# Fused attention and SwiGLU block: the front of batches 0 and 1 reordered, with VectorE sums for two denominators

## The chip, the core and the metric

The kernel runs on one core of a Trainium2 chip. A core has five engines with instruction queues of their own: TensorE (PE: matmuls and, beside them, weight loads, PEld), VectorE (DVE), ScalarE (ACT), GpSimd (POOL) and SyncE (SP). Each works its queue in order; an instruction starts when its turn has come and when everything that it waits for is there. Transfers run on 16 DMA engines beside them. Nearly all loads here are issued by POOL, since they turn fp32 into bf16 on the way. The metric is the device time of one execution in microseconds (us); less is better.

## The reference

Eight batches of attention over a compressed memory, then a SwiGLU block. Sizes: 8 batches, 8 heads, 576 positions, head size 64, 32 memory slots; 512 model columns, 1536 hidden columns.

```python
a = np.exp(phi - max)                     # [b, h, s, m]
a = a / (a.sum(axis=s) + 1e-09)           # weights of the 32 memory slots
k_m = einsum('bhsm,bhsd->bhmd', a, k)     # compressed keys
v_m = einsum('bhsm,bhsd->bhmd', a, v)     # compressed values
p = softmax(scale * q @ k_m.T)            # over the 32 slots
x = (p @ v_m) as [4608, 512]
out = (silu(x @ w_gate) * (x @ w_val)) @ w_out
```

The denominators of the first softmax can be divided out late (into the scale of the score exponential and of the evacuation of U, below), and so can the maximum be left out.

## The kernel before

**Front.** Batches 0 and 1 are prepared by code written out by hand at the end of the kernel (L880 to L960), in program order for all engines. `phi_exp_masked` writes exp(phi) into a tile `t_mphi` that holds two groups g of partitions, each with zeros in the other's half. `k_items` gives two steps: `denominators` (18 matmuls of one column with a vector of ones, L244, then a reciprocal L262 and its product with the scale, L352, the tile `rk`) and `sums` (36 matmuls L325 by `direct`, then four copies to `t_kT`, L339). `q_items` transposes q on TensorE in three parts (L383), copied to `t_qT` by the engine that a letter names, "v" for VectorE and "a" for ScalarE. `scores` (L396) is followed by four exponentials on ScalarE (L407, scale `rk`). The inverse sum of the second softmax is made by `z_inv` (a matmul L423 with the block matrix `bones`, then Ln, Ln, Exp on ScalarE, L426 and L428). Later batches use another form, `z_inv_v`: on VectorE a transposing sum L435, a reciprocal L442, a transpose L444. `norm` multiplies the exponentials by it (L452, the tile `t_A`). `v_direct` makes the values' part of `t_kT`. `warm(n)` issues matmuls of `bones` with itself (L870, 512 columns each for n = 4) whose results nobody reads, to keep TensorE busy while it would wait.

**Into the hidden layer.** A matmul of the compressed values with a chunk of w_gate or w_val gives U (L472, `u_round`), which is evacuated from PSUM by ScalarE (L494) and VectorE (L498). `gv_gate` multiplies U's gate half with `t_A` (L515, 2 matmuls of 288 columns) and puts Silu on ScalarE (L532); the postponed `mul` does the same with the value half and multiplies on VectorE (L538). `flush_mul(n)` issues n of the postponed ones. `gv_slot` is a gate, then the values that were pending. The hidden columns come in three chunks of 512; chunk 0 comes in two halves ("half chunks" 0 and 1), because its weights are loaded in halves. `u_half(b, which, 0, half, evac)` makes U for half a chunk, with which = (0,) for gates, (1,) for values, (0, 1) for both; evac names the engines for the two PSUM banks.

**Loads.** POOL issues in this order: k0, q0, k1, q1, v0, v1, the weights W of chunk 0 in quarters (gate, value, gate, value), chunk 1 (gate, value), chunk 2 (gate, value), then w_out's first chunk (WO), k2, WO, phi2, WO, v2. phi0 and phi1 are issued by SP and ACT.

**PSUM.** There are 8 banks, handed out from a list in program order: `bank` takes the first, `done` puts one at the end. A matmul therefore also waits until the last reader of its bank has finished.

Of the kernel before, what the change touches and what calls it, by code (L numbers as in the profile page):

```python
# [9 lines left out]
FP32 = mybir.dt.float32  # L10
BF16 = mybir.dt.bfloat16
# [3 lines left out]
def kernel(  # L15
# [135 lines left out]
    def load_wo(c):  # L151
        t = wpool.tile([128, 4, DM], BF16, tag=f"WO{c}", name=f"WO{c}")
        nc.gpsimd.dma_start(
            out=t,
            in_=moe_w_out[c * CH:(c + 1) * CH, :].rearrange("(i p) f -> p i f", p=128),
        )
        for i in range(4):
            WO[4 * c + i] = t[:, i]
        WOc[c] = t


    ident = consts.tile([128, 128], BF16, tag="ident", name="ident")
    bones = consts.tile([128, 128], BF16, tag="bones", name="bones")
    ones1 = consts.tile([128, 1], BF16, tag="ones1", name="ones1")
    ones2 = consts.tile([128, NG], BF16, tag="ones2", name="ones2")


    ephis, rSs, bkvs, kTs, es, atts = {}, {}, {}, {}, {}, {}
# [10 lines left out]
    masked = {}  # L179
# [23 lines left out]
    esums = {}  # L203

    def phi_sum(b):
# [13 lines left out]
        nc.gpsimd.tensor_tensor(out=hl[:, 1], in0=t[:, 0], in1=hl[:, 0], op=ALU.subtract)  # L219
        esums[b] = hl  # L220

    def kv_sum(b, p, parts):


        w0, w1 = parts[0], parts[-1] + 1
        n = (w1 - w0) * D
        for j in range(JK):
            for i in range(NP):
                for g in range(NG):
                    nc.tensor.matmul(  # L230
                        p[g][32 * i:32 * i + 32, 0:n],
                        lhsT=phi_of(b, g, j, i),
                        rhs=kvs[b][64 * g:64 * g + 64, w0:w1, i, j * D:(j + 1) * D],
                        start=(j == 0),
                        stop=(j == JK - 1),
                        tile_position=(64 * g, 32 * i),
                    )

    def kv_denominators(b, p):

        if b in masked:
            for g in range(NG):
                for j in range(JK):
                    nc.tensor.matmul(  # L244
                        p[:, g:g + 1],
                        lhsT=masked[b][:, j, g].rearrange("p i m -> p (i m)"),
                        rhs=ones1,
                        start=(j == 0),
                        stop=(j == JK - 1),
                    )  # L250
            return
        if b in esums:
            hl = esums.pop(b)
            terms = [hl[:, t] for t in range(2)]
        else:
            terms = [ephis[b][:, j].rearrange("p i m -> p (i m)") for j in range(JK)]
        for n, x in enumerate(terms):
            nc.tensor.matmul(p, lhsT=x, rhs=ones2, start=(n == 0), stop=(n == len(terms) - 1))
# [157 lines left out]
    lzs = {}  # L416

    def z_inv(b, g):

        p = gv_banks()  # L420
        lz = att.tile([128, 2, HALF], FP32, tag="lz", bufs=3, name="t_lz")
        for r in range(2):
            nc.tensor.matmul(  # L423
                p[r][:, 0:HALF], lhsT=bones, rhs=es[b, g][:, r], start=True, stop=True
            )
            nc.scalar.activation(out=lz[:, r], in_=p[r][:, 0:HALF], func=AF.Ln)  # L426
        done(*p)
        nc.scalar.activation(out=lz, in_=lz, func=AF.Exp, scale=-1.0)  # L428
        lzs[b, g] = lz
# [17 lines left out]
        )  # L447
        lzs[b, g] = lz

    def norm(b, g):  # L450
        a = att.tile([128, 2, HALF], BF16, tag=f"A{g}", name="t_A")
        nc.vector.tensor_tensor(out=a, in0=es.pop((b, g)), in1=lzs.pop((b, g)), op=ALU.mult)  # L452
        atts[b, g] = a


# [49 lines left out]
    def flush_mul(n=None):  # L505
        for _ in range(len(pend) if n is None else n):
            pend.pop(0)()
# [316 lines left out]
    def q_items(b, evac):  # L824
        return [lambda n=n: q_T(b, n, evac[n]) for n in range(3)]
# [5 lines left out]
    def u_half(b, which, c, half, evac):  # L831

        return lambda: u_round(b, ((which, c, (half,)),), evac)
# [9 lines left out]
    def run(items):  # L843
        for x in items:
            x()
# [13 lines left out]
    def gv_slots(b):  # L859
        return [lambda s=s: gv_slot(b, s) for s in range(2 * NJF)]  # L860

    def warm(n, narrow=0):


        p = bank([128, DM], FP32, "p_warm")
        x = bones.rearrange("p (a c) -> p a c", a=1)
        sizes = [1] * narrow + [4] * ((n - narrow) // 4)
        sizes += [n - sum(sizes)] if n > sum(sizes) else []
        for a in sizes:
            nc.tensor.matmul(  # L870
                p[:, 0:128 * a],
                lhsT=bones,
                rhs=x.to_broadcast([128, a, 128]) if a > 1 else bones,
                start=True,
                stop=True,
            )
        free.insert(0, held.pop(id(p))[0])
# [6 lines left out]
    load_q(0)  # L884
    load_k(1)
    nc.vector.memset(bones, 0.0)
    nc.vector.memset(ones1, 1.0)
    nc.vector.memset(ones2, 0.0)
    for g in range(NG):
        nc.vector.memset(ones2[64 * g:64 * g + 64, g:g + 1], 1.0)  # L890
# [12 lines left out]
    for c in range(1, NCH):  # L903
        for which in range(2):
            load_w(which, c)
    load_wo(0)
    load_k(2)
    load_wo(1)
    load_phi(2, nc.gpsimd)
    load_wo(2)  # L910
    load_v(2)
    for c in range(NCH):
        u_buffer(1, c, f"S{c}")


    warm(104)
    k0, k1 = k_items(0, "vvvv"), k_items(1, "vvvv")
    q0, q1 = q_items(0, "vav"), q_items(1, "vav")
    run(k0)
    warm(8)  # L920
    run(k1[:1])
    run(q0)
    warm(4)
    scores(0, 0)
    scores(0, 1)
# [1 line left out]
    z_inv(0, 0)  # L927
    run(k1[1:])
    z_inv(0, 1)
    norm(0, 0)  # L930
    warm(12)
    run(q1)
    norm(0, 1)
    warm(8)
    scores(1, 0)
# [1 line left out]
    v_direct(0, "vvvv")  # L937
    z_inv(1, 0)
    warm(8)
    z_inv(1, 1)  # L940
    norm(1, 0)
    warm(16)
    v_direct(1, "vvvv")
    warm(8)
# [1 line left out]

    g0, g1 = gv_slots(0), gv_slots(1)
    nc.scalar.preload_act_table_set("silu_and_others")
    run([u_half(0, (0,), 0, 0, "va")])
    norm(1, 1)  # L950
    run([u_half(0, (1,), 0, 0, "va"), u_half(1, (0, 1), 0, 0, "av")])
    for s in range(4):
        gv_gate(0, s)
    flush_mul(2)
    for s in range(2):
        gv_gate(1, s)
        flush_mul(1)
    run([u_half(0, (0, 1), 0, 1, "va"), u_half(1, (0, 1), 0, 1, "aa")])
    flush_mul(2)
    run(g1[2:4] + g0[4:8] + g1[4:6])  # L960
    for c in range(1, NCH):
        s = 8 * c
        run([u_item(0, c)] + g1[s - (2 if c == 1 else 3):s] + g0[s:s + 5])
# [27 lines left out]
    for b in range(2, B):  # L991
# [59 lines left out]
        g = gv_slots(b)  # L1051
# [61 lines left out]
```

## Time and profile before

| what | value |
|---|---|
| median of the 3 runs shown | 232.75 us (232.64 to 232.76) |
| the profiled execution's own time | 232.59 us |
| its span, first to last instruction | 230.8 us |
| TensorE busy in the span | 222.3 us (96%) |
| VectorE, ScalarE, GpSimd busy | 184.8 us, 171.6 us, 145.1 us |
| read from and written to HBM | 42.47 MB, 9.44 MB |
| granted TensorE clock, mean | 1.000 |

How to read the profile: busy shares are means over the whole span, and the stages differ. A row of the timeline has the start, the length, the engine, the line, the operation, the tiles (out<-in), the shape and the number of instructions; in brackets stands how long the engine was idle before it, and what ended that. "issue" means that nothing in the profile shows the cause. "DMA to landing" is the time from a transfer's issue to the arrival of its last byte. Matmuls overlap one another, so their lengths don't add up; their distance from start to start does.

### The profile page before, as it was taken

Reading aid. Unit: us, or ns where it says so; the run is one execution under the profiler, and the core shown is the slowest. Engines: PE = TensorE matmul, PEld = TensorE weight load, DVE = VectorE, ACT = ScalarE, POOL = GpSimd, SP = SyncE. Lnnn points to the kernel's source line nnn. Section 1 sums busy time; section 2 is a strip of 40 time slices with the busy share of each in tenths; the row PEclk is TensorE's granted clock in tenths of the full one; section 3 lists DMA queues with packets and bytes.
Section 4 is the critical chain, followed back from the end, with each engine's and each line's share of the span. In section 5 each row is a group of like instructions: output and inputs, shape, how many; then the busy total and the mean of one; then the engine's idle time right before and its main releaser. Section 6 shows DMA issues by size and latency. Waiting matters only on the chain.

```text
span 230.8 us, 7191 instructions
## 1 busy us (share of the span) xinstructions
PE 222.3 (96%) x2818; PEld 169.7 (74%) x2818; DVE 184.8 (80%) x423; ACT 171.6 (74%) x365; POOL 145.1 (63%) x197
## 2 busy tenths in 40 slices
PE   6997799999999999999999999999999999999993
PEld 2554476778887777878788787887788778878882
DVE  4056789999976799989997668998999899977832
ACT  2858898988547989968896658978898789677310
POOL 8422427998099759765977689464845394029291
PEclk9999999999999999999999999999999999999999
DMA  6999999999996993999299964996022602202024
GB/s 213 209 211 206 199 207 207 216 250 266 207 210 176 258 257 69 224 204 177 78 214 195 230 137 110 253 231 101 18 76 102 116 0 95 87 7 91 23 93 162
DMA packets 36546, 36.84 MB, mean 160 GB/s; under 512 B 14496, under 2 KB 30880, under 8 KB 36512
## 3 DMA queue, kind: packets, MB, share of 16 engines
q0 software_dynamic: 16272, 22.42, 52.7%
q1 hardware_dynamic: 19712, 13.37, 22.8%
q10 hardware_dynamic: 528, 0.59, 0.8%
q8 instruction: 22, 0.36, 0.6%
q14 instruction: 12, 0.10, 0.1%
HBM read 42.47 MB, written 9.44 MB: 225 GB/s over the span
## 4 chain that ended last, share of the span: by engine, by line
PE 87%; DMA 9%; POOL 2%; issue 0%; DVE 0%; POOLq 0%
PE p_os L723 21%; PE p_g L515 21%; PE p_v L515 20%; PE p_oc L723 10%; DMA W<-in_moe_w_val_dram 9%; PE p_oa L723 5%; PE p_u L472 5%; PE p_kv L230 2%; PE p_g L396 1%; POOL t_kv L99 1%; POOL t_kv L103 1%; PE p_q L383 1%; POOL t_q L108 0%; POOL W L138 0%; DVE t_q L339 0%
## 5 line engine op out<-in xcount | busy, mean ns | idle before, releaser
L538 DVE TENSOR_TENSOR t_h<-t_sg,p_v 128x288 bf16<-128x288 bf16 x192 | 81.7, 451 | 14.3 <-PE p_v L515 7.3
L515 PEld LDWEIGHTS <-t_U 128*128 128x128 bf16 x768 | 73.9, 98 | 21.2 <-issue 3.5
L532 ACT ACTIVATE t_sg<-p_g 128x288 bf16<-128x288 f32 x192 | 73.2, 424 | 17.2 <-PE p_g L515 11.4
L515 PE MATMUL p_g<-t_A,t_U 128*128 128x288 bf16 x384 | 77.0, 286 | 0.0
L515 PE MATMUL p_v<-t_A,t_U 128*128 128x288 bf16 x384 | 76.9, 286 | 0.0
L723 PEld LDWEIGHTS <-t_S 128*128 128x128 bf16 x384 | 37.3, 98 | 4.5 <-issue 0.2
L603 POOL TENSOR_TENSOR t_S<-t_h 128x512 bf16<-128x512 bf16 x17 | 19.6, 1154 | 27.7 <-DVE t_h L538 26.4
L723 PEld LDWEIGHTS <-t_h 128*128 128x128 bf16 x288 | 27.1, 98 | 8.6 <-issue 5.0
L492 ACT CAST t_U<-p_u 128x512 bf16<-128x512 f32 x51 | 27.0, 606 | 6.4 <-PE p_u L472 6.4
L723 PE MATMUL p_os<-t_T,t_S 128*128 128x256 bf16 x192 | 23.7, 273 | 0.0
L560 POOL TENSOR_TENSOR t_S<-t_S,t_h 128x512 bf16<-128x512 bf16 x17 | 19.6, 1155 | 1.3
L560 POOL TENSOR_TENSOR t_S<-t_h 128x512 bf16<-128x512 bf16 x16 | 18.4, 1152 | 0.0
L560 POOL TENSOR_TENSOR t_S<-t_h,t_S 128x512 bf16<-128x512 bf16 x16 | 18.4, 1151 | 0.0
L472 PE MATMUL p_u<-W,t_kT 64*32 64x512 bf16 (+1 forms) x416 | 15.3, 363 | 1.2 <-DMA W<-in_moe_w_val_dram 0.6
L870 PE MATMUL p_warm<-bones 128*128 128x512 bf16 x44 | 13.6, 450 | 1.7 <-DVE bones L892 1.7
L496 DVE CAST t_U<-p_u 128x512 bf16<-128x512 f32 x21 | 13.6, 683 | 1.9 <-PE p_u L472 1.9
L723 PE MATMUL p_os<-t_T,t_h 128*128 128x256 bf16 x96 | 14.8, 273 | 0.0
L452 DVE TENSOR_TENSOR t_A<-t_E,t_lz 128x576 bf16<-128x576 bf16 x16 | 11.4, 739 | 0.7 <-ACT t_lz L428 0.7
L723 PE MATMUL p_oc<-t_T,t_S 128*128 128x256 bf16 x96 | 11.9, 273 | 0.0
L723 PE MATMUL p_oa<-WO,t_h 128*128 128x256 bf16 x96 | 11.8, 273 | 0.0
L723 PE MATMUL p_oc<-WO,t_S 128*128 128x256 bf16 x96 | 11.8, 273 | 0.0
L723 PE MATMUL p_os<-WO,t_h 128*128 128x256 bf16 x96 | 11.8, 273 | 0.0
(108 smaller groups left out, 312.5 us busy)
## 6 DMA issues: line engine op xcount, KB each, us to landing
out_dram<-t_o SPq DMA_DIRECT2D x11, 512.0 KB, 3.3
t_kv<-in_k_dram POOLq DMA_DIRECT2D x8, 576.0 KB, 10.7
t_q<-in_q_dram POOLq DMA_DIRECT2D x8, 576.0 KB, 8.7
t_kv<-in_v_dram POOLq DMA_DIRECT2D x8, 576.0 KB, 15.1
t_phi<-in_phi_dram POOLq DMA_DIRECT2D x6, 576.0 KB, 8.5
out_dram<-t_o SPq DMA_DIRECT2D x10, 256.0 KB, 3.8
WO<-in_moe_w_out_dram POOLq DMA_DIRECT2D x3, 512.0 KB, 19.4
W<-in_moe_w_gate_dram POOLq DMA_DIRECT2D x2, 512.0 KB, 16.5
```

Of the source, the lines that this page charges most:

```text
L230: nc.tensor.matmul(p[g][32 * i:32 * i + 32, 0:n], lhsT=phi_of(b, g, j, i), rhs=kvs[b][64 * g:64 * g + 64, w0:w1, i, j * D:(j + 1) * D], st ...
L452: nc.vector.tensor_tensor(out=a, in0=es.pop((b, g)), in1=lzs.pop((b, g)), op=ALU.mult)
L472: nc.tensor.matmul(p[g][32 * i:32 * i + 32, o:o + n], lhsT=kTs[b][64 * g:64 * g + 64, 2, 32 * i:32 * i + 32], rhs=w_part(w, c, i, g, halve ...
L492: nc.scalar.copy(out=t, in_=p)
L496: nc.vector.tensor_copy(out=t, in_=p)
L515: nc.tensor.matmul(p[:, 0:HALF], lhsT=Us[b, c, g][:, o // 2, which, 128 * (o % 2):128 * (o % 2 + 1)], rhs=atts[b, g][:, r], start=(g == 0) ...
L532: nc.scalar.activation(out=sg, in_=gate[:, 0:HALF], func=AF.Silu)
L538: nc.vector.tensor_tensor(out=dst, in0=sg, in1=val[:, 0:HALF], op=ALU.mult)
L560: eng.tensor_tensor(out=out, in0=x, in1=y, op=ALU.subtract)
L603: eng.tensor_tensor(out=t[:, 0], in0=A21, in1=A22, op=ALU.add)
L723: nc.tensor.matmul(mine[home][:, u], lhsT=lhs(c, m, u), rhs=rhs(c, m), start=fresh and u == 0, stop=(k == 5), skip_group_check=u == 1 or n ...
L870: nc.tensor.matmul(p[:, 0:128 * a], lhsT=bones, rhs=x.to_broadcast([128, a, 128]) if a > 1 else bones, start=True, stop=True,)
```

## The change

It touches only the front.

- `phi_sum_masked`, new: seven VectorE instructions add up exp(phi) of a batch over the 9 blocks j into one 128x128 tile, split into a bf16 high and low part; the denominators are then 2 matmuls in place of 18. It is called for batch 0 before the first `warm`, for batch 1 behind q0's copies. The tile `ones1` goes.
- Batch 0's `sums` come before its `denominators`; batch 1's come behind its `sums` and `z_inv(0, 1)`. All three copies of q1 are VectorE's.
- The first `warm` has 64 in place of 104 and uses `ident`, made by POOL, as its stationary operand, so that it waits for POOL.
- `norm(0, 0)` and `norm(0, 1)` come behind q1's copies, `norm(1, 0)` behind the first U evacuation, and `norm(1, 1)` goes to GpSimd. The inverse sum of batch 1, group 1 is made by `z_inv_v`.
- In half chunk 0 the order is: U gates of batch 0, U gates of batch 1, four gates of batch 0, U values of both, four gates of batch 1, four values. Six gates and four values came before the second half chunk; now there are eight gates and four values.
- Six loads (WO, k2, WO, phi2, WO, v2) move in program order behind `norm(1, 1)`.

```diff
+    def phi_sum_masked(b):
+        u = att.tile([128, JK, NP, M], BF16, tag="ephi", name="t_ephi")
+        e = u.rearrange("p j i m -> p j (i m)")
+        z = masked[b].rearrange("p j g i m -> p j g (i m)")
+        t = att.tile([128, 4, 128], FP32, tag="es", bufs=1, name="t_es")
+        hl = att.tile([128, 2, 128], BF16, tag="ehl", bufs=1, name="t_ehl")
+        for out, x, y, op in (
+            (e, z[:, :, 0], z[:, :, 1], ALU.add),
+            (t, e[:, 0:4], e[:, 4:8], ALU.add),
+            (t[:, 0:2], t[:, 0:2], t[:, 2:4], ALU.add),
+            (t[:, 0], t[:, 0], t[:, 1], ALU.add),
+            (t[:, 0], t[:, 0], e[:, 8], ALU.add),
+            (hl[:, 0], t[:, 0], None, None),
+            (hl[:, 1], t[:, 0], hl[:, 0], ALU.subtract),
+        ):
...
     def kv_denominators(b, p):
-        if b in masked:
-            for g in range(NG):
-                for j in range(JK):
-                    nc.tensor.matmul(
...
-    load_wo(0)
-    load_k(2)
-    load_wo(1)
-    load_phi(2, nc.gpsimd)
-    load_wo(2)
-    load_v(2)
...
-    warm(104)
+    phi_sum_masked(0)
+    warm(64, lhs=ident)
     k0, k1 = k_items(0, "vvvv"), k_items(1, "vvvv")
-    q0, q1 = q_items(0, "vav"), q_items(1, "vav")
-    run(k0)
+    q0, q1 = q_items(0, "vav"), q_items(1, "vvv")
+    run(k0[1:])
     warm(8)
-    run(k1[:1])
+    run(k0[:1])
+    warm(8)
     run(q0)
+    phi_sum_masked(1)
     warm(4)
     scores(0, 0)
     scores(0, 1)
@@
     z_inv(0, 0)
     run(k1[1:])
     z_inv(0, 1)
-    norm(0, 0)
+    run(k1[:1])
     warm(12)
     run(q1)
+    norm(0, 0)
     norm(0, 1)
     warm(8)
     scores(1, 0)
@@
     v_direct(0, "vvvv")
     z_inv(1, 0)
     warm(8)
-    z_inv(1, 1)
-    norm(1, 0)
+    z_inv_v(1, 1)
     warm(16)
     v_direct(1, "vvvv")
     warm(8)
@@
-    run([u_half(0, (0,), 0, 0, "va")])
-    norm(1, 1)
-    run([u_half(0, (1,), 0, 0, "va"), u_half(1, (0, 1), 0, 0, "av")])
+    run([u_half(0, (0,), 0, 0, "av")])
+    norm(1, 1, nc.gpsimd)
+    load_wo(0)
+    load_k(2)
+    load_wo(1)
+    load_phi(2, nc.gpsimd)
+    load_wo(2)
+    load_v(2)
+    norm(1, 0)
+    run([u_half(1, (0,), 0, 0, "aa")])
     for s in range(4):
         gv_gate(0, s)
-    flush_mul(2)
-    for s in range(2):
+    run([u_half(0, (1,), 0, 0, "vv"), u_half(1, (1,), 0, 0, "aa")])
+    for s in range(4):
         gv_gate(1, s)
-        flush_mul(1)
+    flush_mul(4)
     run([u_half(0, (0, 1), 0, 1, "va"), u_half(1, (0, 1), 0, 1, "aa")])
-    flush_mul(2)
-    run(g1[2:4] + g0[4:8] + g1[4:6])
+    flush_mul(4)
+    run(g0[4:8] + g1[4:6])
```

More of the change, by code (lines that the diff above doesn't have):

```diff
@@ L163 @@
     bones = consts.tile([128, 128], BF16, tag="bones", name="bones")
-    ones1 = consts.tile([128, 1], BF16, tag="ones1", name="ones1")
     ones2 = consts.tile([128, NG], BF16, tag="ones2", name="ones2")
@@ L220, in phi_sum @@
         esums[b] = hl
+    def phi_sum_masked(b):
[13 more added lines that the diff above has]
+        ):
+            if y is None:
+                nc.vector.tensor_copy(out=out, in_=x)
+            else:
+                nc.vector.tensor_tensor(out=out, in0=x, in1=y, op=op)
+        esums[b] = hl
     def kv_sum(b, p, parts):
@@ L239, in kv_denominators @@
     def kv_denominators(b, p):
-        if b in masked:
-            for g in range(NG):
-                for j in range(JK):
-                    nc.tensor.matmul(
[L245 to L251, printed above, removed]
         if b in esums:
@@ L448, in z_inv_v, with norm @@
         lzs[b, g] = lz
-    def norm(b, g):
+    def norm(b, g, eng=nc.vector):
         a = att.tile([128, 2, HALF], BF16, tag=f"A{g}", name="t_A")
-        nc.vector.tensor_tensor(out=a, in0=es.pop((b, g)), in1=lzs.pop((b, g)), op=ALU.mult)
+        eng.tensor_tensor(out=a, in0=es.pop((b, g)), in1=lzs.pop((b, g)), op=ALU.mult)
         atts[b, g] = a
@@ L860, in gv_slots, with warm @@
         return [lambda s=s: gv_slot(b, s) for s in range(2 * NJF)]
-    def warm(n, narrow=0):
+    def warm(n, narrow=0, lhs=None):
         p = bank([128, DM], FP32, "p_warm")
@@ L871, in warm @@
                 p[:, 0:128 * a],
-                lhsT=bones,
+                lhsT=bones if lhs is None else lhs,
                 rhs=x.to_broadcast([128, a, 128]) if a > 1 else bones,
@@ L886 @@
     nc.vector.memset(bones, 0.0)
-    nc.vector.memset(ones1, 1.0)
     nc.vector.memset(ones2, 0.0)
```

## The prediction

> **What bounds the kernel now.** I read the slices first, then TensorE's waits, then the timeline from 0 to 66 us with the landing times of single loads.
>
> The 40 slices are 5.77 us each:
>
> ```profile
> PE   6997799999999999999999999999999999999993
> DVE  4056789999976799989997668998999899977832
> DMA  6999999999996993999299964996022602202024
> ```
>
> TensorE is full from the sixth slice (28.9 us) to the end, and below that only in the front; the DMA engines are full from the second slice to the twelfth. TensorE's idle times over the whole span say the same:
>
> ```profile
> PE p_warm L870 <- DVE bones L892: 1.7, 1, 1.7
> PE p_g L396 <- DVE t_qT L339: 0.9, 2, 0.5
> PE p_mT L325 <- DMA t_kv<-in_v_dram: 0.7, 1, 0.7
> PE p_u L472 <- DMA W<-in_moe_w_val_dram: 0.6, 1, 0.6
> PE p_u L472 <- DVE t_kT L339: 0.6, 1, 0.6
> ```
>
> The same question for 27 to 231 us returns no wait at all. So the end moves by as much as TensorE's work moves in the front, and by nothing else; behind the front the change leaves the work as it was. I take as mark the point from which both kernels have the same work left: the U matmuls of chunk 1, batch 0.
>
> ```profile
> 25.73 0.30 PE L472 MATMUL p_u<-W,t_kT 64*32 64x256 bf16 x8 [0.58 <-DVE t_kT L339]
> 26.66 0.52 PE L472 MATMUL p_u<-W,t_kT 64*32 64x256 bf16 x24 [0.63 <-DMA W<-in_moe_w_val_dram]
> 27.12 1.16 PE L515 MATMUL p_g<-t_A,t_U 128*128 128x288 bf16 x8
> ...
> 34.84 0.40 PE L472 MATMUL p_u<-W,t_kT 64*32 64x512 bf16 x8
> ```
>
> The last row is the mark: the value half of chunk 1 starts at 34.84 (its gate half at 34.62). Now the loads that these rows need:
>
> ```profile
> 6.01 0.76 POOL L138 DMA_DIRECT2D W<-in_moe_w_gate_dram  x1
> 6.74 0.77 POOL L138 DMA_DIRECT2D W<-in_moe_w_val_dram  x1
> 17.67 0.74 POOL L138 DMA_DIRECT2D W<-in_moe_w_val_dram  x1 [1.99 <-DMA t_q<-in_q_dram]
> ```
>
> Their landing times are 19.6, 19.9 and 16.9 us: they land at 25.6 (gates, first quarter), 26.6 (values) and **34.6** (values of chunk 1). The other two quarters land at 9.30 + 18.7 = 28.0 and 12.11 + 17.2 = 29.3. The stretches from 8 to 44 us move 201 to 214 GB/s each, so the queue is the limit, and the change removes nothing in front of these loads. **The ceiling**: the mark can move from 34.84 to about 34.64 (0.04 us behind the landing, as 26.66 is behind 26.62 in the chain of waits). At most 0.2 us can be won, however well the front goes.
>
> **The change part by part.**
>
> *Sums on VectorE.* The trace doesn't show them. Nearest rows: a bf16 add of 128x512 takes 0.42 us (L560), an add with fp32 of the same size 0.69 (L753), so with 288 columns at 0.45 (L538) a fixed 0.14 us, 0.54 ns an element in bf16 and 1.07 in fp32. One sum: 1152 elements bf16 0.76; 512 to fp32 0.69; 256 fp32 0.41; three of 128 at 0.28; the cast 0.25 (a copy of 128 takes 0.28 from PSUM); six gaps of 0.03 between dependent instructions: 3.15 us. Upper bound: the first add at the fp32 rate, 1.37, gives 3.8; lower bound: no gaps and half the small ones' fixed part, 2.6. I take 3.15, the bf16 row being the nearest. The 36 one-column matmuls that go (2 x 0.59 us) lay in TensorE's waiting time: nothing is won.
>
> *VectorE's chain.* These rows are the load that it carries already:
>
> ```profile
> 11.46 1.21 DVE L339 CAST t_kT<-p_mT 64x128 bf16<-64x128 f32 x4 [0.32 <-PE p_mT L325]
> 13.00 1.23 DVE L339 COPY t_qT<-p_q 128x768 bf16<-128x768 bf16 x2
> 19.59 0.75 DVE L452 TENSOR_TENSOR t_A<-t_E,t_lz 128x576 bf16<-128x576 bf16 x1
> 21.71 0.98 DVE L339 CAST t_kT<-p_mT 64x64 bf16<-64x64 f32 x4 [1.38 <-PE p_mT L325]
> 24.64 0.98 DVE L339 CAST t_kT<-p_mT 64x64 bf16<-64x64 f32 x4 [0.49 <-PE p_mT L325]
> ```
>
> After the change it starts when batch 0's exponentials end (5.85 + 2 x 1.18 = 8.2): sum 11.4; k0 copies 12.65; reciprocal and product 13.05; q0 copies 14.25; sum 17.4; k1 copies 18.65; reciprocal 19.05; three q1 copies (0.475 apart, 0.56 the last) 20.6; two norms 0.67 apart 21.9; v0 copies 22.95; z_inv_v (by the rows of later batches L435 0.76, L442 0.27, L444 0.78, and gaps) 24.85; v1 copies **25.85**, against 25.62 before. It hardly waits: batch 1's scores start at 20.65 (19.72 before), their exponentials end near 22.7, in time for 22.95. So VectorE becomes the bound of the front, and ends within 0.25 us of where it did. ScalarE loses Ln, Ln, Exp of one group (1.3 us), its table load ends before 25.7.
>
> *The first warm-up* starts when ident is there (4.02) instead of at 1.74: 16 matmuls. Before, 12 of them were 0.43 apart until 6.83 and the rest 0.21; the same course ends at 4.05 + 12 x 0.43 + 4 x 0.21 = 10.05. k0's sums (0.76) then end before 11.4, when VectorE is free.
>
> The Trainium skill speaks against this one: "TensorE: Matmul & The Clock Gate", Part 1, says that the clock is released after a busy window of about 3.4 us that runs freely. This trace shows 5.1 us (1.74 to 6.83), which lies between one window and two. By the page the release may come as late as 10.9, k0's copies at 11.7, and VectorE's chain at 26.1; that would add some 0.1 us to the estimate.
>
> *Gates ahead of values.* U gates of batch 0 start at 25.73 as before (load at 25.6); both evacuations end at 26.6 (0.48 from 26.12). Batch 1's U gates start at 25.95, behind the v1 copies. The four gates start at 26.68 instead of 27.12, so 0.44 is won, and take 8 x 0.1225 = 0.98 to 27.66. Then come the U values that used to stand ahead of them: a switch of tile shape each way (0.09 each, from the start distances of 0.216 at 29.67 and 0.2 at 30.24) and 2 x 0.11: batch 1's gates start at 28.07. Before, the same work is done at 28.11. **The gain is spent there.** Eight units of 0.245 (four gates, four values) end at 30.03, U of half chunk 1 starts at 30.14.
>
> *ScalarE.* It now evacuates five of the eight U banks:
>
> ```profile
> 26.12 0.47 ACT L494 ACTIVATE t_U<-p_u,t_rS 128x256 bf16<-128x256 f32 x1 [0.15 <-PE p_u L472]
> 27.06 1.05 ACT L494 ACTIVATE t_U<-p_u,t_rS 128x256 bf16<-128x256 f32 x2 [0.46 <-PE p_u L472]
> 28.00 1.94 ACT L532 ACTIVATE t_sg<-p_g 128x288 bf16<-128x288 f32 x6
> ```
>
> The six Silus are 0.3 apart (1.94 less one length of 0.43, over five). New order: three evacuations 0.37 apart from 26.13, four Silus from 27.25, two evacuations from 28.41, four Silus from 29.15, the last ending at 30.45. Batch 1's U of half chunk 1 needs that last bank: it starts at 30.52, not 30.36, a wait of 0.16. VectorE's evacuation stands behind four products and ends at 31.8, which holds the next gate by 0.05. Fifteen units remain (seventeen before): 30.83 + 15 x 0.245 + 0.05 + 0.09 = 34.65 for the mark's gate half, against 34.62.
>
> *norm(1, 1) on GpSimd.* By its rows (1.15 for 512 bf16, 0.73 for 256 fp32) 1.3 to 1.65 us from 24.95: done by 26.6, needed at 28.07; the cover is 1.5 us. Behind it in POOL's queue stand the six moved loads; WO is issued at 26.3 to 26.7 instead of 25.88. W of chunks 1 and 2 keep the queue full until 39.8, and the first of the six is read at 54.07 (landing 42.3 before). The nearest user is q2, behind them: landing 42.62 + 16.2 = 58.8, read at 59.04; it moves only if the queue runs dry, which it doesn't.
>
> A second rule against: "GPSIMD Engine Reference", section 8, says that GpSimd shares its SBUF interfaces with VectorE, and that two-input VectorE instructions contend. The trace has it: L560 takes 0.64 to 0.66 beside POOL copies at 55.3, 0.42 otherwise. But L603 beside a POOL load issue (54.48 to 55.24) takes 0.42 as well, and only such issues lie beside the new sums; by the rule alone each sum would be 0.4 longer (half as much again over the 0.74 of an issue), VectorE's end 26.65, and the time 0.6 more.
>
> **The sum**: +0.03 us at the mark, nothing behind it. On the profiled execution's 232.59 (span 230.8 and 1.8 around it) that is 232.62; the median of the runs is 0.16 higher, so 232.8.
>
> **The rivals.**
>
> 1. *The ceiling is reached.* If ScalarE's and VectorE's small waits (0.16, 0.05) vanish, the mark stops at the landing at 34.6: -0.2, **232.55**. For it: both rest on 0.1 us of my estimates.
> 2. *VectorE's chain is late* (slower). Place: v1 copies and the evacuation of U behind them. Batch 1's U gates have 0.2 us of cover, from 25.85 to 26.05; from there each tenth goes to the end. Price: sums at 3.8 end the chain at 27.15, +1.1: **233.85**. For it: VectorE carries 17.4 us of work in 17.6 (8.25 to 25.85), so that each wait for TensorE or ScalarE adds up. Against: bf16 adds on strided tiles run at 0.42 in the trace.
> 3. *The weights land earlier*, faster by more than 0.2%. v0 took 3.47 us behind q1 (17.4 to 20.87), where its neighbours take 2.7 to 2.8. Without that all later landings come 0.65 earlier; batch 1's U gates, which wait for VectorE's end at 25.85, then let batch 0's gates start at 26.2 and not 26.68, so about 0.45 is won: **232.3**. Nothing in the change acts on that queue.
> 4. *The array falls back to its slow rate* before 25.7, as fewer matmuls fill the front: 5.1 us at half speed, +2.5, **235.3**. Against: the longest gap that I find, 0.75 ahead of batch 1's scores (19.9 to 20.65), is no longer than the idle times of before.
>
> That the change doesn't do what it says is my forecast itself: gates do start earlier, and TensorE isn't further along.
>
> **How the numbers follow.** A difference of 0.2% (0.47 us) is about what a measurement of this kernel can tell from no change. Forecast 0.50, rival 1 0.14, both within it. Rival 2 0.24, of which 0.03 stays within. Rival 3 0.09, of which 0.01 stays within. Rival 4 0.03. Within: 0.50 + 0.14 + 0.03 + 0.01 = 0.68; slower: 0.21 + 0.03 = 0.24; faster 0.08. The range, 232.3 to 233.9, reaches to rival 3 and to the upper bound of the sums; rival 4 and the outer parts of 2 and 3 stay out.
>
> **What would show it.** Right: gates at about 26.7, U values behind them near 27.75, batch 1's gates at 28.1, the mark at 34.6 to 34.9, VectorE without idle time from 8.3 to 25.9. Wrong: a first add near 1.4 us, v1 copies ending behind 26.1, chunk 1's values landing well away from 34.6, or TensorE waits behind 35 us.

## The result, and the profile after

| | before | after |
|---|---|---|
| median (22 executions each) | 232.75 us | 233.19 us |
| lowest and highest | 232.48, 233.17 | 232.47, 235.91 |
| ratio after to before | | 1.0033 (95%: 1.0020 to 1.0046) |
| profiled execution, span | 232.59, 230.8 us | 232.56, 230.8 us |
| TensorE busy, matmuls | 222.3 us, 2818 | 220.6 us, 2776 |
| VectorE busy | 184.8 us | 191.7 us |

The median is 0.39 us above the predicted 232.8 and inside the range; the medians lie 0.19% apart, but the ratio of the executions, 1.0033 with an interval from 1.0020, is past the 0.2% that I called no change. The ratios leave out executions over 1.5% above the fastest of their kernel (one each in e1 and e9, three in e4); medians and counts take all. But the shape of the result is not what I forecast. The kernel before spreads over 0.7 us. After the change 12 executions lie between 232.47 and 233.22, where the forecast put them, and 10 between 233.69 and 235.91. I call an execution of over 233.5 us **long**. In two of the 10 (233.69 and 233.94) the span is 231.2 and 230.7 us, so that their extra time lies outside it, and nothing below explains it; the other 8 have spans of 232.1 to 234.1. The profiled execution of after is a short one.

Its slices, as those shown of before (PE, DVE, DMA):

```profile
PE   2987999999999999999999999999999999999993
...
DVE  4598889999976799989997668998999899977832
...
DMA  6999999999996993999199945995023502202024
```

VectorE is fuller from the second slice to the fifth, where the sums stand; TensorE is emptier in the first, where the warm-up now starts later, and from the sixth on it looks as before. TensorE's waits over the whole span of after:

```profile
PE p_warm L880 <- POOL ident masks.py:199: 4.1, 1, 4.1
PE p_g L406 <- DVE t_qT L349: 0.9, 2, 0.5
PE p_mT L335 <- DMA t_kv<-in_v_dram: 0.8, 2, 0.7
```

The two waits at U, for the value weights and for `t_kT`, are gone, and from 28 us on there is none, as predicted. (Lines of after are 10 higher than those of before: L482 is L472, L525 is L515; in e8 and e12 they are 14 higher.) The timeline of TensorE in the front of after (start, length):

```profile
25.52 0.86 PE L482 MATMUL p_u<-W,t_kT 64*32 64x256 bf16 x16
26.41 1.23 PE L525 MATMUL p_g<-t_A,t_U 128*128 128x288 bf16 x8
27.57 0.41 PE L482 MATMUL p_u<-W,t_kT 64*32 64x256 bf16 x16
27.91 1.15 PE L525 MATMUL p_g<-t_A,t_U 128*128 128x288 bf16 x8
...
29.97 0.89 PE L482 MATMUL p_u<-W,t_kT 64*32 64x256 bf16 x32
...
34.58 0.62 PE L482 MATMUL p_u<-W,t_kT 64*32 64x512 bf16 x16
```

The gates start 0.71 us before those of the old kernel (27.12), and the last row, the gate half of the mark, stands 0.04 before (34.62). The gain is made and spent, as said. A short execution of after takes what the kernel before takes.

**Where the long ones lose.** The first experiment is the changed kernel once more, and its profiled execution took 234.74 us. Its waits of TensorE behind 40 us:

```profile
PE p_u L482 <- DMA t_kT<-t_bkv: 1.2, 1, 1.2
PE p_v L525 <- ACT t_sg L542: 0.3, 1, 0.3
```

Here is the loss, at 110 to 113 us, seventy microseconds behind everything that the change touches: against before, TensorE is 0.27 us late at the mark, 0.31 at 103.5 us, and is 2.07 late at 115 us and 2.16 at its end. What it waits for is a DMA transpose that SyncE issues behind another. SyncE's rows, first in the short execution of after:

```profile
100.20 6.07 SPq L117 DMA_TRANSPOSE t_qT<-t_q  x1
106.38 1.84 SPq L294 DMA_TRANSPOSE t_kT<-t_bkv  x1
```

then in the long one:

```profile
100.54 8.00 SPq L117 DMA_TRANSPOSE t_qT<-t_q  x1
108.64 1.85 SPq L294 DMA_TRANSPOSE t_kT<-t_bkv  x1
```

The first column is the start, the second how long the issue held the queue. The transpose of q held it 1.93 us longer, so `t_kT` is issued later and lands at 113.21 instead of 110.63. TensorE wants it at 111.17, with 0.54 us of cover (0.46 in before; in e5 none was left, and TensorE lost 0.11 us there). And the lateness starts earlier, in the loads of batch 5, issued by POOL at 91.2 to 93.6. The DMA view from 88 to 110 us, with the time from issue to landing (us) in the last column, of the short execution:

```profile
t_q<-in_q_dram POOLq DMA_DIRECT2D x1, 576.0 KB, 5.4
...
t_kv<-in_v_dram POOLq DMA_DIRECT2D x1, 576.0 KB, 11.2
```

and of the long one:

```profile
t_q<-in_q_dram POOLq DMA_DIRECT2D x1, 576.0 KB, 7.2
...
t_kv<-in_v_dram POOLq DMA_DIRECT2D x1, 576.0 KB, 14.8
```

So in a long execution q of batch 5 already needs 1.8 us more.

The two transposes aren't behind these loads by a dependency. They belong to batch 4: the program has SyncE issue five transposes of q, for batches 3 to 7, and this is the second; its q was loaded at 72.6 and had landed at 79.0. They go beside the loads of batch 5. In all 14 profiled executions the issue of this transpose ends 0.0 to 1.8 us behind the landing of batch 5's v, which comes at 104.3 to 109.3: a late v and a long hold go together. And the lateness isn't spread over the whole load. The DMA view of the long execution from 105 to 108.3 us:

```profile
q1 hardware_dynamic: 656, 0.32, 123.0%
q8 instruction: 1, 0.02, 5.9%
q0 software_dynamic: 19, 0.02, 3.6%
```

q0 carries POOL's loads. 3.6% of 16 engines' time is 0.6 of one engine's: most of v is there, and its last packets trickle in, less than one in flight on average, while in the short execution no packet of q0 stands between 104.5 and 108. The second long execution that was profiled, e4's, has the same (4.0% from 105.5 to 109.2).

The question for the experiments was what a change before 32 us has to do with a load at 91 us.

### The profile page after: what moved, and what is told of

Its sections match the earlier page's. It is cut to its first block, busy times and chain, and to the rows that moved or that the text cites. A ratio compares the mean times of both kernels' runs of the same rounds, so it can differ in the third digit from the quotient of the medians.

```text
span 230.8 us, 7120 instructions
## 1 busy us (share of the span) xinstructions
PE 220.6 (96%) x2776; PEld 167.8 (73%) x2776; DVE 191.7 (83%) x439; ACT 170.5 (74%) x363; POOL 146.6 (64%) x198
## 4 chain that ended last, share of the span: by engine, by line
PE 88%; DMA 7%; DVE 2%; POOL 1%; issue 0%; POOLq 0%
PE p_g L525 21%; PE p_os L733 21%; PE p_v L525 20%; PE p_oc L733 10%; DMA t_kv<-in_v_dram 7%; PE p_u L482 6%; PE p_oa L733 5%; PE p_kv L251 2%; PE p_g L406 1%; POOL t_kv L99 1%; DVE t_kT L349 1%; PE p_q L393 1%; POOL t_q L108 0%; DVE t_z L445 0%; DVE t_lz L454 0%
## 5 line engine op out<-in xcount | busy, mean ns | idle before, releaser
L525 PEld LDWEIGHTS <-t_U 128*128 128x128 bf16 x768 | 73.8, 98 | 21.3 <-issue 3.5
L525 PE MATMUL p_g<-t_A,t_U 128*128 128x288 bf16 x384 | 76.6, 286 | 0.0
L525 PE MATMUL p_v<-t_A,t_U 128*128 128x288 bf16 x384 | 76.3, 286 | 0.0
L482 PE MATMUL p_u<-W,t_kT 64*32 64x512 bf16 (+1 forms) x416 | 16.0, 364 | 0.1
L602 POOL COPY t_x<-t_h 128x256 bf16<-128x256 bf16 x24 | 11.6, 491 | 0.0
L758 ACT COPY t_q<-p_os 128x512 f32<-128x512 f32 (+1 forms) x10 | 5.4, 540 | 7.0 <-DVE t_o L349 4.0
```

The source lines that it names most:

```text
L482: nc.tensor.matmul(p[g][32 * i:32 * i + 32, o:o + n], lhsT=kTs[b][64 * g:64 * g + 64, 2, 32 * i:32 * i + 32], rhs=w_part(w, c, i, g, halve ...
L525: nc.tensor.matmul(p[:, 0:HALF], lhsT=Us[b, c, g][:, o // 2, which, 128 * (o % 2):128 * (o % 2 + 1)], rhs=atts[b, g][:, r], start=(g == 0) ...
L602: nc.gpsimd.tensor_copy(out=xs[b // 2][:, 4 * c:4 * c + 4, :, b % 2].rearrange("p o (t r) -> p o t r", r=2), in_=hts[b, c].rearrange("p o ...
L758: nc.scalar.copy(out=t, in_=mine[home])
```

## The experiments

"Mark" is TensorE's lateness against before at the U of chunk 1 (its value half), and the packet (explained below) is the one nearest to batch 5's loads, in us; both are read from the one profiled execution of each kernel.

| run | median us | ratio (95%) | mark | instruction packet at | long |
|---|---|---|---|---|---|
| before, all runs | 232.59 to 232.75 | 1 | 0 | 88.4 | 1 of 130 |
| after | 233.19 | 1.0033 (1.0020 to 1.0046) | -0.04 | 91.8 | 10 of 22 |
| e1 after, again | 233.93 | 1.0037 (1.0015 to 1.0059) | +0.27 | 91.9 | 8 of 12 |
| e2 after, old first warm-up | 233.28 | 1.0034 (1.0017 to 1.0051) | -0.16 | 90.0 | 4 of 12 |
| e3 before, new first warm-up | 233.03 | 1.0018 (1.0009 to 1.0027) | +0.33 | 88.5 | 1 of 11 |
| e4 after, old order of gates | 233.74 | 1.0037 (1.0012 to 1.0062) | +0.28 | 92.4 | 7 of 12 |
| e5 after, 42 more matmuls | 232.65 | 1.0000 (0.9991 to 1.0009) | +0.13 | 88.8 | 0 of 11 |
| e6 before, 78 more | 232.76 | 1.0018 (0.9995 to 1.0041) | +0.20 | 91.9 | 1 of 11 |
| e7 before, new order of gates | 232.95 | 1.0010 (1.0001 to 1.0018) | +0.34 | 89.0 | 0 of 11 |
| e9 after, 128 more | 232.86 | 1.0020 (0.9997 to 1.0043) | +0.05 | 91.9 | 3 of 12 |
| e10 after, 42 more elsewhere | 232.71 | 1.0003 (0.9995 to 1.0012) | -0.05 | 88.7 | 0 of 12 |
| e11 before, 69 more | 232.75 | 1.0024 (1.0000 to 1.0047) | +0.09 | 92.1 | 3 of 12 |

(e8 and e12 delay VectorE on purpose and stand apart, below. Four chips were used: one for e1 to e4, a second for e5 to e8, a third for e9 to e11, a fourth for e12, with executions of before on each.)

**The same kernel again (e1).** No edit.

> The changed kernel once more, unaltered. Its 22 runs spread from 232.47 to 235.91 us, those of the kernel before only from 232.48 to 233.17. Theory C (clock): the first warm-up starts 2.3 us later and is 10 matmuls shorter, so that in some executions TensorE runs at half rate again or still when the dense work begins; expected: half of the runs at 232.4 to 232.9, the others 0.6 to 3.5 us above, and in a slow run's trace the start distance of 512-column matmuls stays 0.43 or returns to it (0.21 otherwise). Theory V (VectorE without slack): late landings of q1, v0 or v1 in some executions go straight to the end; expected in a slow run's trace: v1 copies ending behind 26.1, TensorE's distances unchanged.

Measured: 4 of 12 at 232.36 to 232.56, 8 at 233.76 to 236.92. The spread belongs to the kernel; the profiled execution, a long one, is the trace read above. It has neither theory's sign: 512-column matmuls are 0.22 us apart from 8.2 us on and the granted clock is 1.0 (against C), and the v1 copies end at 26.00 (against V).

**The old first warm-up in the new kernel (e2).**

```diff
-    warm(64, lhs=ident)
+    warm(104)
```

> The changed kernel with the first warm-up of before: warm(104) with bones, from about 1.74 us. Theory C: the spread goes, all runs within 232.4 to 232.9, median near 232.6, 0.1 below the kernel before. Theory V: the spread stays as in the changed kernel (median near 233.2, runs up to 234.5).

Measured: 8 of 12 at 232.81 to 233.49, 4 at 234.15 to 234.88, all with a mean granted clock of 0.997 or more. The long executions stay, so that the warm-up's length and the clock behind it are not their cause. The profiled execution shows another small loss: TensorE is 0.14 us ahead until 226 us, yet the span is 231.2. An instruction packet (explained below) lies at 227.4 beside the last stores, whose two issues hold SyncE's queue 1.83 us instead of 1.27.

**The new first warm-up in the old kernel (e3), and the old order of gates in the new one (e4).**

```diff
 e3, in before:
-    warm(104)
+    warm(64, lhs=ident)
 e4, in after (half chunk 0 as before the change):
-    run([u_half(0, (0,), 0, 0, "av")])
+    run([u_half(0, (0,), 0, 0, "va")])
...
-    run([u_half(1, (0,), 0, 0, "aa")])
+    run([u_half(0, (1,), 0, 0, "va"), u_half(1, (0, 1), 0, 0, "av")])
```

> The kernel before with only the first warm-up of the change: warm(64) with ident, from about 4.05 us. Theory C: the spread appears, some runs 0.6 to 3.5 us above 232.7. Theory V: no spread, 232.5 to 233.1, as VectorE has 8 us of idle time in this front.

> The changed kernel with the order of before in half chunk 0 (U gates, U values, then gates and values interleaved); front, sums and warm-up as changed. Step of the prediction: the gates' earlier start is spent again by 28.1, so the fast runs should be within 0.15 us of the changed kernel's fast runs (232.5 to 232.8). Theories C and V both leave the spread as it is (runs up to 234.5).

Measured: the median of e3 is 0.33 us above that of before, with one long execution of 11 (233.69, granted clock 0.989); e4 has 7 of 12. In both the first value quarter of W landed late, at 26.95 and 26.90 instead of 26.62, and in the profiled executions the old order passes that on one to one: the mark is 0.33 and 0.28 late. In the trace of after the same quarter landed at 27.26, and the mark is not late at all. This is what the new order of gates is worth there: it takes the value quarter off the path. It isn't needed for the long executions.

**A second theory.** What differs between the kernels with long executions and those without is the number of instructions. The profile lists a DMA queue "instruction", q8, with packets of 16384 bytes, 22 of them in before and 21 in after. TensorE's list has 5636 matmuls and weight loads in before, 5552 in after: 5636 over 22 packets is 256 a packet (5552 over 21 is 264), so the 84 instructions that the change removes (42 matmuls and their weight loads) would move every later packet. The 42 are the 36 one-column matmuls, 8 of the warm-ups and 2 of `z_inv`, less 4 new ones. The DMA view of before, from 87.5 to 90 us (packets, MB, share of the 16 DMA engines' time):

```profile
q8 instruction: 1, 0.02, 2.6%
```

has a packet there at 88.4, and none from 91 to 93. After has none at 88, and from 91 to 93 us this:

```profile
q0 software_dynamic: 13, 0.06, 34.2%
q8 instruction: 1, 0.02, 3.4%
```

The packet runs from 91.75 to 92.85 us, over the first packets of batch 5's q (from 92.45). (A second such queue, q14, has 12 packets of 8192 bytes; around these loads they stand at 87.9 and 108.7 us in after, 88.2 and 108.8 in e5, 88.1 and 108.4 in e10, so that they don't tell the kernels with long executions from those without.) The next runs test the place of q8's packets: the same work with other numbers of instructions. A warm-up of 512 columns in one matmul is cut into four of 128 columns; the trace shows nearly the same time a column (0.43 us for 512 and 0.107 for 128 before the clock is up, 0.216 and 0.056 after).

**After with the old number of instructions (e5, e10).**

```diff
 e5:
-    warm(64, lhs=ident)
+    warm(64, narrow=56, lhs=ident)
 e10, seven later warm-ups, first one unchanged:
-    warm(8)
+    warm(8, narrow=8)
...
```

> The changed kernel, whose first warm-up of 64 blocks is cut into 58 matmuls (56 of 128 columns, 2 of 512) in place of 16 of 512, with the same columns and results nobody reads. TensorE's instruction stream has then as many rows as the kernel before (5638; the changed kernel has 5554, 42 matmuls and 42 weight loads fewer). Theory F (instruction fetches: TensorE's stream is read in 16 KB packets by one of the 16 DMA engines that carry the loads; the 84 missing rows move such a packet from 88.4 to 91.8 us, onto the start of batch 5's loads, and in about half of the executions q5, v5 and the transposes behind them land 1.5 to 3.5 us late, so that TensorE waits at 104 to 113 us): packets at 88 to 89 and near 101 us again, all times within 232.2 to 233.0, median 232.5, no second group. Theory S (the slower executions come from the new work itself, its VectorE sums or the later loads of the second half of the list, and not from the place of the packets): the two groups stay, with about half of the times at 233.7 to 234.8, median near 233.2. Theory C (TensorE's clock after a short first warm-up) was already spoken against by the run with the old warm-up; it would give two groups here as well, with a granted clock under 1.0 in the late ones.

> The changed kernel with its 42 more matmuls not in the first warm-up, which stays 16 matmuls of 512 columns, but in the seven behind it (56 blocks of 128 columns in 56 matmuls in place of 14). TensorE's rows as many as before the change (5638). Theory F: packets at 88 to 89 us again, no second group, all times within 232.3 to 233.1, median 232.6. Rival G': the cure of the run with 58 matmuls was the first warm-up's cutting: the second group is back here, a third to a half at 233.7 to 235, median above 232.9.

Measured: the packet is back at 88.8 and 88.7 us, and the long executions are gone: 0 of 23, where after and e1 had 18 of 34. It does not matter which warm-up is cut. The unpadded kernel was not run on these two chips; what was, with the packet at 91.9 to 92.1, follows. Both kernels, with all parts of the change in, take what before takes: 1.0000 and 1.0003, and neither interval reaches past 0.12%. That is what the forecast said of the change.

**After with a whole packet more (e9).**

```diff
-    warm(64, lhs=ident)
+    warm(64, narrow=64, lhs=ident, halves=40)
-    warm(8)
+    warm(8, narrow=8)
...
```

> The changed kernel, all of whose warm-ups are cut into smaller matmuls (128 columns each, 40 of the first 64-block warm-up's matmuls 64 columns): 128 matmuls and 128 weight loads more with the same columns, so 256 rows more on TensorE, one instruction packet more in front, and the later packets at the same distance from the work as in the changed kernel itself (about 91.8 us, on the start of batch 5's loads at 91.2 to 92.5). Theory F (the place of the packets): the second group comes back, a third to a half of the times at 233.7 to 235, median 232.8 to 233.7, in spite of the padding. Rival G (it is not the place: any finer cutting of the warm-ups cures it, by TensorE's clock or by the later start of the front): no second group, as with 42 more, all times within 232.4 to 233.1.

`halves`, a parameter added to `warm`, gives so many matmuls of 64 columns; the first warm-up has 84 matmuls then, and all later ones are cut like the second. Measured: packet at 91.9 us, 3 of 12 long (234.58, 235.28, 236.95). The cutting itself is no cure: 3 of 12 against 0 of 12 in e10 on the same chip. The share is under the third to a half that I expected.

**The old kernel with its packets moved (e6, e11).**

```diff
 e6, in before:
-    warm(104)
+    warm(104, narrow=104)
 e11, in before:
-    warm(104)
+    warm(104, narrow=92)
```

> The kernel before, whose first warm-up of 104 blocks is cut into 104 matmuls of 128 columns in place of 26 of 512, with the same columns. 78 matmuls and 78 weight loads more; against a packet of some 256 rows this puts the later packets where 100 rows fewer would put them, near 92 us as in the changed kernel (84 fewer: 91.8). Nothing else of the change is in. Theory F: a second group appears in the kernel before, with TensorE waiting for the transposed k at 104 to 113 us: a third to a half of the times at 233.7 to 235, median 232.9 to 233.6. Theory S: no second group, all times within 232.4 to 233.3, median 232.75.

> The kernel before with its first warm-up in 95 matmuls (92 of 128 columns and 3 of 512) in place of 26: 69 more, 138 rows, which against 256 rows a packet stands for 118 rows fewer. With 78 more the packet lay at 91.85 to 92.78 and batch 5's first bytes began at 92.74, so that they hardly met, and 2 of 11 executions were long. Here the packet should lie some 0.3 to 0.7 us later and overlap the first bytes of that load, as in the changed kernel. Theory F: a second group in the kernel before, a third to a half of the times at 233.7 to 235.9. Theory S (the new work of the change itself is needed for the second group): none, or one stray as with 78, median 232.7.

Measured: e6 puts the packet at 91.85 to 92.78 and q's first bytes start at 92.74; one execution of 11 is long (235.84; the expectation of e11 counts 233.33 as a second). That is a miss for theory F, which had a third to a half. e11 puts it at 92.1, and 3 of 12 are long (233.59, 234.86, 235.57, the last two with a clock of 0.985 and 0.992), again under the share expected; the kernel before as it is had 1 of 130. So long executions can be had without any part of the change. Over all runs: packet at 88 to 89 us, 2 long of 175; at 90.0 to 92.4, 36 of 93. Of these, 0 and 28 have a granted clock of 0.997 or more. On the third chip alone, where both kernels ran with the packet early and late, 0 of 41 and 6 of 24 are long.

**The new order of gates alone (e7).**

```diff
 in before, half chunk 0 as after the change:
-    run([u_half(0, (0,), 0, 0, "va")])
+    run([u_half(0, (0,), 0, 0, "av")])
...
```

> The kernel before with one part of the change alone: the new order of half chunk 0 (gates of batch 0, gates of batch 1, four gates, then the values) with its engines for the evacuations; sums of exponentials, warm-up, norms and the list of loads as before. TensorE has as many rows as before. By the prediction's working the gates start some 0.4 us earlier and the gain is spent by 28.1 us, mark within 0.05 of 34.84: median 232.6 to 232.8. If the order also absorbs a late load of the first value quarter (as the changed kernel's trace suggests, where it landed at 27.26 in place of 26.62 and the mark did not move), the mark goes no further than the landing of chunk 1's values allows, 0.2 at most: 232.5. If the order costs by itself (bank waits on ScalarE): 233.0. Theory F: no second group; theory S puts the cause in the other parts, and has no second group either, unless the order is the cause.

Measured: 232.95, no long execution. In the profiled one the first gate quarter of W landed at 25.92 (25.59 before), U starts at 26.06, the gates at 26.95 and the mark at 34.96, 0.34 late. The gates start 0.17 earlier than before and the work to the mark takes 8.01 us (7.50 in before, 8.17 in after): the order costs 0.5 to 0.7 us of its own and pays only if the gates start that much earlier. In e7 and in after the gates start 0.89 us behind U (26.06 and 25.52); the 0.54 between the two is the landing of the first gate quarter (25.92 and 25.38), so that e7 doesn't show whether the order needs the rest of the change.

**How much cover VectorE's chain has (e8), and the clock (e12).** In the kernel of e5 the sum of batch 1 does its first two additions twice:

```diff
             (t, e[:, 0:4], e[:, 4:8], ALU.add),
+        ) + ((
+            (e, z[:, :, 0], z[:, :, 1], ALU.add),
+            (t, e[:, 0:4], e[:, 4:8], ALU.add),
+        ) if b == 1 else ()) + (
```

> The changed kernel with the padded warm-up (as the run with 58 matmuls), in which the sum of batch 1 does its first two VectorE additions twice (0.76 and 0.69 us and two gaps: 1.52 us more on VectorE's chain, results unchanged). The changed kernel's trace has 0.61 us of VectorE idle time ahead of the copies of v0, so the copies of v1 should end some 0.9 later, near 26.9 in place of 26.03. The prediction's rival 2 said that batch 1's U gates have cover until 26.05 and that each tenth behind that goes to the end: mark near 35.45, time 0.85 above that of the padded kernel, about 233.35. If the gates that now stand ahead of the values, or the wait for the value weights (landing 27.0 to 27.3), still cover it: 0.3 or less. If VectorE's chain is no bound at all: 0.

Three rows of it, from the timelines of TensorE, VectorE and TensorE:

```profile
18.21 0.51 PE L272 MATMUL p_S<-ones,t_ehl 128*128 128x2 bf16 x2 [1.64 <-DVE t_ehl L242]
```

```profile
25.64 0.98 DVE L353 CAST t_kT<-p_mT 64x64 bf16<-64x64 f32 x4
```

```profile
35.16 0.62 PE L486 MATMUL p_u<-W,t_kT 64*32 64x512 bf16 x16
```

The v1 copies end at 26.62, 0.57 behind the 26.05 at which the prediction ended their cover, and the mark stands at 35.16, 0.54 behind that of before. One to one, from that point, in this execution; the copies had been expected to end near 26.9. The transpose at 111 us adds 0.44 more: its result landed at 112.13, and with TensorE 0.55 late it was wanted at 111.74. That makes 1.0 us in the profiled execution (233.58, against 233.35 expected). The median is 234.97, though (ratio 1.0087, 1.0062 to 1.0113), for four of the six took 234.72 to 235.63, with a mean granted clock of 0.993, where the other two had 1.0: 0.007 of 231 us are 1.6 us. The first of the rows above offers a reason, an idle stretch of TensorE of 1.64 us, though the execution that it is from has a clock of 1.0.

```diff
 e12, in the kernel of e8 (first warm-up: narrow=48):
     z_inv(0, 1)
+    warm(24)
     run(k1[:1])
```

> The kernel with the sum of batch 1 made 1.52 us longer, in which 6 further warm-up matmuls of 512 columns (1.3 us at 0.21 apart) stand where TensorE was idle from 16.56 to 18.21 us; the first warm-up gives 6 matmuls back, so that TensorE's rows stay 5638 and the packets at 88 to 89 us. In the run without them 4 of 6 times were 234.7 to 235.6 with a mean granted clock of 0.993 and 2 were 233.6 to 233.9 with 1.0; 0.007 of 231 us are 1.6 us, which is the distance. Theory T (prediction's rival 4: the idle stretch lets the clock fall back for some microseconds in most executions): no clock of 0.993, all times 233.2 to 233.9, median 233.4. Rival (the idle stretch has nothing to do with it): half or more of the times at 234.7 and above with 0.993 again, median above 234.

Measured: 233.73 (ratio 1.0039, 1.0028 to 1.0050), all 11 executions at 233.44 to 234.06 and clock 0.997 or more in each; the median is 0.33 above the 233.4 expected. So the idle stretch is the likely reason: it isn't proved, since e12 ran on another chip than e8 and no execution with 0.993 was profiled. This is the prediction's rival 4, in a place that the change as it is keeps filled.

## Why the prediction was right and wrong, step by step

- **The bound and the mark.** Right. No wait of TensorE behind 28 us in the short execution; predicted 34.65 for the mark's gate half, measured 34.58. Chunk 1's values landed at 34.55 (34.6 assumed), and the mark's value half followed at 34.80: the ceiling was not reached. That the median lies in the range is luck, though: the range reached up to 233.9 for a late chain on VectorE, and what moved the median is something else (last point).
- **The sum on VectorE.** Right to 1%: 3.15 us predicted, 3.18 measured, each term within 0.03 us (three of them in these rows, the two first additions and the 256 elements with the first of the 128s):

```profile
8.24 0.76 DVE L240 TENSOR_TENSOR t_ephi<-t_mphi 128x1152 bf16<-128x1152 bf16 x1 [3.75 <-ACT t_mphi L187]
9.04 0.69 DVE L240 TENSOR_TENSOR t_es<-t_ephi 128x512 f32<-128x512 bf16 x1
9.77 0.75 DVE L240 TENSOR_TENSOR t_es<-t_es 128x256 f32<-128x256 f32 x2
```

  The last row holds two, 0.42 and 0.29. The rule on shared SBUF interfaces (Trainium skill, "GPSIMD Engine Reference", section 8) would have made it 0.4 longer by the prediction's estimate; both sums took 3.18 with a POOL load issue beside them (9.28 and 14.92), so issues don't bring that contention here.
- **VectorE's chain.** The end was predicted at 25.85 and came at 26.03, 0.02 before the cover ends. "It hardly waits" was wrong by one wait: 0.61 us for v0's sums, since v0 landed at 21.27 instead of 20.87. The mechanism and its price (rival 2) hold in e8's profiled execution. That the chain lies so close to its limit was luck as much as working.
- **The first warm-up.** Predicted to end at 10.05, measured 10.18. The rate doubled 5.07 us after its start. Other executions show 2.5 us (e10), 3.0 (e8) and 5.5 (e5): the single course that I copied from before is one of several. The Trainium skill, "TensorE: Matmul & The Clock Gate", Part 1, says that the point varies since the window runs freely; but 2.5 and 3.0 us are under its window of about 3.4, and the spread of 3 us is above its 0.5 us either way. That the end came within 0.13 us was luck. e5's 5.5 us cost nothing (ratio 1.0000); a release at 10.9, which I feared, is in no trace.
- **Gates ahead of values.** The start was mis-sized (26.68 predicted, 26.41 measured; 0.21 of the 0.27 is the first gate quarter, landed at 25.38 and not at 25.6), and so was what the new order costs (0.47 against 0.67: 0.1 more at the switch to the U values, 27.39 to 27.57, and 0.28 instead of 0.16 at ScalarE's bank, 30.20 to 30.48). The two errors cancel. That the gain is spent was right, the place was not: at batch 1's gates, where I had it gone, 0.2 of it was left (27.91 against 28.11). e7 shows the cost with a smaller gain.
- **norm on GpSimd.** 1.28 us from 25.18 (1.3 to 1.65 from 24.95): within its cover.
- **"+0.03 us at the mark, nothing behind it."** This is the step that failed, in its second half: 10 of 22 executions lie 0.9 to 3.2 us above before's median of 232.75. The first half is -0.04. Behind it, the change takes 84 instructions from TensorE's list. I counted the one-column matmuls as time, found that they lay in a wait, and put them at nothing. They also set where the instruction packets fall among the loads, 60 us later. With the packet there, about half of the executions of after and e1 (18 of 34) are long; in the two long ones profiled (e1, e4) batch 5's loads are late, and beside them batch 4's transposes of q and of k, one behind the other in SyncE's queue, of which the second has only 0.54 us of cover.

**What stays open.** That a packet at 90 to 92.4 us goes with long executions is shown by moving it both ways, in both kernels, for the old one by 4 long executions of 23. That this packet is the one that matters isn't shown: all behind it move too (101.2 and 107.7 us in before, 106.1 and 109.6 in after). How it delays the load is argued. The Trainium skill, "DMA: Bandwidth & Descriptors", section "Queues, rings and completion order", says that a DMA engine takes turns between its queues packet by packet; the trickle at the end of v fits one engine that is late, but the trace doesn't name the engine of a packet, so that it can't be seen whether the one that carries the instructions is the one that is late. The packet takes about 1 us and q comes 1.8 to 2.5 us late; the difference is unexplained, and so is why the overlap harms some executions and not others: in the profiled ones of after, e9 and e11 it did nothing. In e2 the packet ends at 91.1, before q's first bytes at 92.3, and 4 of 12 are long all the same. Why the old kernel suffers less often (4 of 23 in e6 and e11) than the new one (18 of 34) isn't settled either; it may be the chip, for on the third chip both have 3 of 12 (e11 and e9). Ten of the 38 long executions in the table also show a clock of 0.985 to 0.993; only in e8 was its cause tested.

## What to carry to other kernels

Removing instructions that cost no time can still move the time: in this kernel the instruction packets are fetched among the loads, and a different number of instructions puts them beside other loads. When a kernel that was tight spreads into two groups after a small edit, look for the wait in a long execution, follow it back to the transfer (and check by the program which batch a transfer belongs to), and pad the instruction list in some idle place before believing any story on the edit itself. And when a sum says "nothing behind this point", ask which chains there have less than a microsecond of cover (here `t_kT` of batch 4, with 0.5).

## What the runs showed of the hardware that I had not expected

- Instruction packets of 16384 bytes, some 256 TensorE instructions each (5636 over 22), take 0.9 to 2.2 us in the short executions and 3.1 in one place of a long one (106.3 us in e1). In these runs they fall into the same microseconds as the loads, and their place depends on how many instructions stand ahead of them.
- In the kernel whose TensorE idles 1.64 us at 16.6 us (e8), the mean granted clock was 0.993 in 4 of 6 executions and 1.0 in the other two, the profiled one among them; with that stretch filled by six matmuls (e12, another chip) it was 0.997 or more in all 11. The idle stretch of 1.22 us at 112 us in e1 goes with 1.0.
- The time until TensorE's rate doubles differs from execution to execution, 2.5 to 5.5 us, with a first warm-up that starts at 4.08 to 4.09 in each (e10, e5).
- A matmul of 128 columns with a weight load of its own costs nearly as much a column as one of 512 (0.056 and 0.216 us a matmul), so instructions can be added to a warm-up for next to nothing: e5 and e10 have 42 more matmuls at ratios of 1.0000 and 1.0003.
